# Turning a pass's sums with VectorE instead of TensorE in a three-layer FP32 kernel, with smaller stores and three small moves

## Chip, cores and metric

One core of one Trainium2 chip. The metric is the device time of one execution in microseconds (us), lower is better; the number quoted is the median of the executions shown. Times inside a profile count from the start of the profiled span.

## What is computed

Three layers in FP32, one behind the other; cut to the arithmetic:

```python
# q, k, v: [4, 8, 576, 64], g_norm: [64]
kv  = einsum('bhsd,bhse->bhde', k, v)
o   = einsum('bhsd,bhde->bhse', q, kv)
x   = o / sqrt(mean(o*o, -1) + 1e-6) * g_norm     # -> [2304, 512]
h   = x @ w_in                                    # w_in  [512, 2048]
x   = (h * clip(h + 3, 0, 6) / 6) @ w_out         # w_out [2048, 512]
p   = probs / (probs.sum(-1) + 1e-9)              # probs [2304, 4]
out = sum(p[:, e] * (relu(x @ w1[e]) @ w2[e]) for e in range(4))
# w1 [4, 512, 1024], w2 [4, 1024, 512]
```

## The kernel before

**Precision.** A product is computed as three products of high and low parts, so operands of the matmuls exist twice (`xh`/`xl`, `gH`/`gL`; the two halves of `so`, `tt`, `win`). Parts are made by one ScalarE copy and one VectorE subtraction (`split`, L813 and L814).

**Attention** (`for i in range(NHB)`, eight steps of half a batch each; its first lines are set in a hand-written order under `manual_schedule`). Work on the weights of the second layer is cut into small "conversion parts" (ScalarE copies and VectorE subtractions) that `conv(SLOTS[i])` puts behind step i. After the eight steps come the first products of the second layer (`first_out`), and in front of them four idle 128x128 products of the identity (L586) whose result is not used. Then a short list of second-layer units runs with `conv(NC.pop(0))` behind each, and the domain probabilities are loaded (L615) and normalised by some small VectorE operations (L617 to L630).

**Second layer** (`step`, `second`). While TensorE computes it, `blocks()` reads `w1` and `w2`, forms their sums and differences and parts, and writes them to DRAM as `dwin`, `dtw` and `dwo`. At unit 20 `turn_probs` turns the probabilities on TensorE and writes them to `dpt`.

**Third layer.** Three passes over 768 tokens each; a pass goes through eight groups `g` (numbered 0 to 23 through the passes). A group has two *fronts* k = 2g and 2g+1 and seven *backs* (g, s), s = 0 to 6, of a product scheme with seven instead of eight products. A front has seven products p1, p6, p2, p5, p7, p3, p4 (in this order) of six matmuls of 128x384, between the operands `xs` and one weight load `win` (1.8 MB, two buffers: load k+2 goes out when p4 of front k is done, L967). They go into two PSUM banks, `qa` and `qb` by turns; VectorE and ScalarE take them out, apply the relu and the probabilities and leave `ar`. `prep` makes the back's operand `so` from `ar` (four buffers, one ScalarE copy and one VectorE subtraction of 128x768, and for some backs a VectorE sum before that). A back is 12 matmuls with one `tt` tile (0.5 MB, fed by L974 as tiles come free) into one of the slots `sx`, `sy`, `sz`; `add_out` (L901, L899) adds the slot to the pass's sums `acc2`, which hold output columns in partitions and tokens along the row. Back (g, 0) also has its slot copied to another one by ScalarE (L1085).

**Flush.** At the end of a pass the sums must be turned, so that tokens lie in partitions, and stored. `flush` does this for one quarter (three tiles of tokens, 256 columns) at a time, four times at each of the two boundaries between passes: behind backs s = 2, 5, 6 of the pass's last group (g = 7, 15) and back s = 0 of the next one (g = 8, 16). It issues six TensorE transposes (L919) into a slot, two ScalarE copies into buffers `done` (L923) and six stores of 64 rows by 256 columns (L911). The third pass ends otherwise: its last group turns the sums inside the final products and stores whole rows.

**What sets the order.** In the third layer the instructions are put in order on each engine by the language's scheduler, which has its own idea of costs; the source gives only dependences and a rough order. Every engine then works through its list in order. All loads of this layer and the stores of the flushes go through one queue, SP's (SyncE's). In the built program, each transfer on this queue waits, besides for its data or buffer, for the landing of the transfer that stands eight places ahead of it.

Of the kernel before, what the change touches and what calls it, by code (L numbers as in the profile page):

```python
# [11 lines left out]
AF = mybir.ActivationFunctionType  # L12
# [5 lines left out]
def kernel(  # L18
# [18 lines left out]
    nc = tc.nc  # L37
    B, H, S, D = q.shape
# [471 lines left out]
    nc.scalar.activation(out=gcol, in_=three, func=AF.Sqrt)  # L510
    att_load(1)
    load_raw()
    SLOTS = {0: 7, 1: 2, 2: 3, 3: 0, 4: 2, 5: 1, 6: 3, 7: 0}
    nop = lambda: None
    engines = {
        mybir.EngineType.PE, mybir.EngineType.Activation, mybir.EngineType.DVE, mybir.EngineType.SP}
    with tc.manual_schedule(engines=engines):
# [64 lines left out]
            return lambda: nc.scalar.activation(out=acc[0][:, o, :], in_=po, func=AF.Copy)  # L582

        acc[0] = accp.tile([P, KD, TB], F32, tag="acc", name="acc1")
        for _ in range(4):
            nc.tensor.matmul(kvp[:, 0, :P], lhsT=ident, rhs=ident, start=True, stop=True)  # L586
        d0 = [first_out(o, kvp[:, o]) for o in range(2)]
        for x in d0:
            x()
# [12 lines left out]
        done[0] = True  # L602
        attps.close()
        psb = banks.enter_context(tc.tile_pool(name="psb", bufs=1, space=bass.MemoryType.PSUM, reuse_waits="tile"))
        NC = [4, 4, 4, 3, 3, 0]
        for kind, t in (("o", 1), ("i", 3), ("o", 2), ("i", 4), ("o", 3), ("o", 4)):
            if kind == "i":
                ff_in(0, t, 0)
            else:
                for _ in ff_out(0, t, 0):  # L610
                    pass
            conv(NC.pop(0))
            if t == 2:
                for y in range(2):
                    nc.sync.dma_start(  # L615
                        out=dp[half[y]], in_=moe2_domain_probs.rearrange("(b s j) e -> s b j e", b=B, j=CJ))
        nc.vector.tensor_reduce(out=psum_e, in_=dp, axis=AX.X, op=ALU.add)  # L617
        nc.vector.tensor_scalar(out=psum_e, in0=psum_e, scalar1=1e-9, scalar2=None, op0=ALU.add)
        nc.vector.reciprocal(out=psum_e, in_=psum_e)
# [10 lines left out]
                in1=psum_e[h, y::2, CJ - 1:].to_broadcast([D, 2, E]), op=ALU.mult)  # L630

    TC = DM // 2
    experts = [(e, j) for e in range(E) for j in range(FP)]
    NG = len(experts) // 2
    INPASS = [3, 5, 7, 9, 11, 13]
# [28 lines left out]

    turns = [0]

    def blocks(k, h):

        r = rawt[k, h]
        last = k - 2 * NG + 2 if h else -1  # L670

        def new():
            turns[0] += 1
            z = ring[turns[0] % len(ring)]
            if not isinstance(z, str):
                return z
            return cvp.tile([P, 2, TC], F32R, tag=z, bufs=2 if z == "r" else 1, name="tb")

        def keep(m, src, low, n=2):
            high = new()  # L680
            low = low if low is not None else new()
            hi, lo = high[:, :n], low[:, :n]
            if src is None:
                src = lo.bitcast(F32)
            elif not h:
                hi, lo = (x.rearrange("p m (c f) -> p (m c) f", c=2) for x in (hi, lo))
            nc.scalar.activation(out=hi, in_=src, func=AF.Copy)
            nc.vector.tensor_tensor(out=lo, in0=src, in1=hi.bitcast(F32), op=ALU.subtract)
            for y, x in ((0, high), (1, low)):
                if not h:  # L690
                    nc.sync.dma_start(
                        out=dwin[k][:, y, m:m + n].rearrange("p m c f -> p m (c f)"), in_=x[:, :n].bitcast(F32))
                    continue
                c = min(n, 7 - m) if m else 1
                nc.sync.dma_start(out=dtw[k // 2][:, m:m + c, k % 2, y], in_=x[:, :c].bitcast(F32))
                if last >= 0 and m < 2:
                    nc.sync.dma_start(
                        out=dwo[last][:, int(m > 0), y].rearrange("p (c d) -> p c d", c=2), in_=x.bitcast(F32))

        def sub(out, a, b, op=ALU.subtract):  # L700
            nc.vector.tensor_tensor(out=out, in0=a, in1=b, op=op)

        odd = new()
        od = odd.bitcast(F32)
        if h:
            sub(od, r[:, 1::2], r[:, 0:2])
        else:
            q = r.rearrange("p c (i f) -> p i c f", i=2)
            a11, a12, a21, a22 = (q[:, i, 2 * c:2 * c + 2] for i in range(2) for c in range(2))
            o4 = od.rearrange("p m (c f) -> p m c f", c=2)  # L710
            sub(o4[:, 0], a21, a22, ALU.add)
            sub(o4[:, 1], o4[:, 0], a11)
        yield
        even = new()
        ev = even.bitcast(F32)
        if h:
            sub(ev[:, 0], r[:, 3], od[:, 0])
            sub(ev[:, 1], r[:, 2], ev[:, 0])
        else:
            e4 = ev.rearrange("p m (c f) -> p m c f", c=2)  # L720
            sub(e4[:, 0], a11, a21)
            sub(e4[:, 1], a12, o4[:, 1])
        yield
        keep(3, None, odd)
        yield
        keep(5, None, even)
        yield
        if h:
            keep(1, r[:, 2:4], None)
        else:  # L730
            keep(0, q[:, 0], None)
        yield
        if not h:
            keep(2, a22, None, 1)
        elif last >= 0:
            keep(0, r[:, 0:2], None)
        else:
            keep(0, r[:, 0:1], None, 1)
        rawt.pop((k, h))
        load_rawt()  # L740
        yield
# [27 lines left out]
    for n in range(NB, N3 + 1):  # L769
        step(n)  # L770
        second(n)
        if n == 20:
            turn_probs()
    assert not stream

# [111 lines left out]
    def slot_tile(name):  # L887
        z = slots[0] % 10
        slots[0] += 1
        return (gp if z < 8 else rp).tile([P, TB], F32, tag=("gH", "gL")[z % 2] if z < 8 else "r", name=name)  # L890
# [9 lines left out]
            else:  # L900
                nc.vector.tensor_tensor(out=a, in0=ps[:, d, :TH], in1=a, op=ALU.add)  # L901

    def store(n, src, cols, last=False):
        for y in range(2):
            if n < B * HH:
                b, a = divmod(n, HH)
                j = 4 * (a % 2) + a // 2 + 2 * y
            else:
                b, j = 2 * (n - B * HH) + y, CJ - 1
            queue = nc.scalar if y and last else nc.sync  # L910
            queue.dma_start(  # L911
                out=out.rearrange("(b s j) d -> b j s d", b=B, j=CJ)[b, j][:, cols], in_=src[half[y]])

    def flush(p, th, c, slot):

        part = acc2.pop((th, c))
        for i in range(3):
            for d in range(2):
                nc.tensor.transpose(  # L919
                    slot[:, i // 2, ((i % 2) * 2 + d) * P:((i % 2) * 2 + d + 1) * P], part[d][:, i * P:(i + 1) * P], ident)  # L920
        for i0, n in ((0, 2), (2, 1)):
            t = slot_tile("done")
            nc.scalar.activation(out=t[:, :n * TC], in_=slot[:, i0 // 2, :n * TC], func=AF.Copy)  # L923
            for i in range(n):
                store(rows[p][3 * th + i0 + i], t[:, i * TC:(i + 1) * TC], slice(c * TC, (c + 1) * TC))

    def product(k, bank, m, first):
        n = 0
# [192 lines left out]
    for g in range(NG2 - 1):  # L1121
        nxt = ahead + front(g + 1, 1)
        if (g + 2) % NG == 0 and g + 2 < NG2:
            b = build((g + 2) // NG)
            bld = {2: "5-", 4: "6-", 7: 1, 9: 6, 10: 2, 12: 5, 13: "7-", 15: 7, 16: 3, 17: "4-", 18: 4}
        else:
            bld = {z - 14: m for z, m in bld.items() if z > 13}
        ci = convert_in(2 * g + 3, *halves) if 2 * g + 3 in INPASS else iter(())
        for s in range(7):
            if s < 5:  # L1130
                prep(g, s + 2)
            back(g, s)
            for z in BEHIND[s]:
                nxt[z]()
                if z in bld:
                    b[bld[z]]()
                if z % 2:
                    next(ci, None)
            if g % 2 and s == 3:
                load_probs(g // 2 + 2)  # L1140
            if g % NG == NG - 1 and s in (2, 5, 6):
                flush(g // NG, *((0, 0), (1, 1), (1, 0))[s - 4 if s > 4 else 0], sz if s == 6 else sx)
            if g % NG == 0 and g and s == 0:
                flush(g // NG - 1, 0, 1, sz)
            if s == 5 and g + 1 < NG2 - 1:
                prep(g + 1, 0)
        if g == NG - 1:
            for _ in range(2):
                room(accp, "acc", 2)
        if g + 1 < NG2 - 1:  # L1150
            ahead = front(g + 2, 0)
            ahead[0]()
            prep(g + 1, 1)
# [22 lines left out]
    for z, (jj, i, f) in enumerate(order):  # L1176
# [10 lines left out]
        r = slot_tile("done")  # L1187
        for y in range(2):
            cols = slice(y * TC, (y + 1) * TC)
            if y:  # L1190
                nc.scalar.activation(out=r[:, cols], in_=ps[i][:, cols], func=AF.Copy)
            else:
                nc.vector.tensor_copy(out=r[:, cols], in_=ps[i][:, cols])
        store(rows[NPASS - 1][i], r, slice(0, DM), True)


# [28 lines left out]
```

## Time and profile before

| what | value |
|---|---|
| median of 3 runs | 1172.46 us (1172.0 to 1173.09) |
| the profiled execution | 1172.47 us, of which its span is 1170.7 us |
| TensorE (PE) busy | 1157.8 us, 99% |
| VectorE (DVE) busy | 914.8 us, 78% |
| ScalarE (ACT) busy | 515.2 us, 44% |
| DMA | 279 MB, mean 239 GB/s |

A page of the profile gives busy time by engine, the span in slices, the chain of work that ended last (followed back from the last instruction to whatever released each step), and groups of instructions by source line. Other views list single instructions in a stretch (timeline), what a line's instructions waited for, busy time by stretch (windows) and the transfers with their time from issue to landing. A matmul's record in a timeline is about 0.16 us longer than the distance to the next, since matmuls overlap: distances between starts are what counts.

### The profile page before, as it was taken

The page shows a single profiled execution, that of the slowest core. Times are in us where ns is not written, and L with a number is a line of the kernel's source. Part 1 is how long each engine was busy: PE and PEld are TensorE (multiplying, and loading weights), DVE is VectorE, ACT ScalarE, POOL GpSimd, SP SyncE. Part 2 cuts the span into 40 slices and gives each one's busy share as a digit, 9 for nine tenths or more (in the row PEclk, how much of TensorE's full clock was granted, in tenths as well). Part 3 has the DMA queues.
Part 4 walks back from the last instruction along what each step waited for, and adds up shares of the span by engine and source line. Part 5 has one row for each costly group of instructions (what it writes and reads, how often), then busy time and mean ns, then how long its engine had stood idle before and what let it go on. Part 6 is the DMA issues. An engine that isn't in the chain of part 4 may idle for free.

```text
span 1170.7 us, 19129 instructions
## 1 busy us (share of the span) xinstructions
PE 1157.8 (99%) x7351; PEld 1082.2 (92%) x7351; DVE 914.8 (78%) x1602; ACT 515.2 (44%) x907; POOL 7.6 (1%) x15
## 2 busy tenths in 40 slices
PE   8999999999999999999999999999999999999998
PEld 6788888888888889999999999999999999999996
DVE  5889999977897854788888896777778867777773
ACT  6877555644555532433333444333334443333321
POOL 1100000000000000000000000000000000000000
PEclk9999999999999999999999999999999999999999
DMA  8723267488599552587878789777777887777821
GB/s 313 248 76 115 87 229 282 137 272 262 179 345 379 211 193 94 201 286 272 283 273 295 271 301 327 262 261 268 253 268 252 282 299 273 252 266 252 289 80 54
DMA packets 117219, 279.24 MB, mean 239 GB/s; under 512 B 10176, under 2 KB 69640, under 8 KB 110728
## 3 DMA queue, kind: packets, MB, share of 16 engines
q1 hardware_dynamic: 116644, 277.24, 69.1%
q8 instruction: 58, 0.95, 0.3%
q10 hardware_dynamic: 484, 0.79, 0.2%
q14 instruction: 33, 0.27, 0.1%
HBM read 212.41 MB, written 65.57 MB: 237 GB/s over the span
## 4 chain that ended last, share of the span: by engine, by line
PE 93%; DVE 3%; DMA 2%; ACT 1%; issue 0%; ACTq 0%; SPq 0%; DVEq 0%
PE slot L1078 29%; PE po L402 16%; PE qa L932 15%; PE qb L932 15%; PE ph L367 5%; PE ph L368 5%; PE ph L369 5%; PE slot L1182 1%; DMA kin<-in_k_dram 1%; DMA vin<-in_v_dram 1%; DMA qin<-in_q_dram 1%; DVE xl L323 1%; PE slot L919 0%; PE kvp L254 0%; PE zp L500 0%
## 5 line engine op out<-in xcount | busy, mean ns | idle before, releaser
L1078 PE MATMUL slot<-so,tt 128*128 128x384 f32 x1932 | 362.2, 334 | 0.0
L1078 PEld LDWEIGHTS slot<-so,tt 128*128 128x128 f32 x1932 | 337.0, 188 | 0.0
L932 PE MATMUL qa<-xs,win 128*128 128x384 f32 x1008 | 202.7, 335 | 0.2 <-ACT qa L1016 0.2
L932 PE MATMUL qb<-xs,win 128*128 128x384 f32 x1008 | 201.9, 334 | 0.0
L402 PE MATMUL po<-gH,w 128*128 128x512 f32 (+1 forms) x632 | 191.0, 368 | 0.2 <-ACT gH L383 0.2
L901 DVE TENSOR_TENSOR acc<-slot,acc 128x384 f32<-128x384 f32 x252 | 128.6, 551 | 63.3 <-PE slot L1078 63.1
L932 PEld LDWEIGHTS qa<-xs,win 128*128 128x128 f32 x1008 | 176.9, 188 | 0.9 <-ACT qa L1016 0.5
L932 PEld LDWEIGHTS qb<-xs,win 128*128 128x128 f32 x1008 | 176.9, 188 | 0.3 <-DVE ar L1011 0.2
L813 ACT ACTIVATE so<-ar 128x768 fp32r<-128x768 f32 x142 | 119.4, 844 | 99.3 <-PE slot L1078 52.9
L814 DVE TENSOR_TENSOR so<-ar,so 128x768 fp32r<-128x768 f32 x142 | 133.9, 953 | 25.8 <-ACT so L813 24.6
L402 PEld LDWEIGHTS po<-gH,w 128*128 128x128 f32 x632 | 115.6, 188 | 20.4 <-ACT gH L383 0.6
L367 PE MATMUL ph<-xh,w 128*128 128x512 f32 (+1 forms) x320 | 118.6, 371 | 0.1
L368 PE MATMUL ph<-xl,w 128*128 128x512 f32 (+1 forms) x320 | 117.9, 368 | 0.0
L369 PE MATMUL ph<-xh,w 128*128 128x512 f32 (+1 forms) x320 | 117.8, 368 | 0.0
L402 PE MATMUL po<-gL,w 128*128 128x512 f32 (+1 forms) x316 | 116.4, 368 | 0.0
L380 ACT ACTIVATE r<-ph,three 128x512 f32<-128x512 f32 (+1 forms) x80 | 51.1, 639 | 57.2 <-PE ph L369 56.4
L381 DVE SCALAR_TENSOR_TENSOR r<-r,ph 128x512 f32<-128x512 f32 (+1 forms) x80 | 50.4, 630 | 30.1 <-ACT r L380 29.7
L367 PEld LDWEIGHTS ph<-xh,w 128*128 128x128 f32 x320 | 60.3, 188 | 10.9 <-DVE r L381 0.5
L369 PEld LDWEIGHTS ph<-xh,w 128*128 128x128 f32 x320 | 60.3, 188 | 10.0
L368 PEld LDWEIGHTS ph<-xl,w 128*128 128x128 f32 x320 | 60.3, 188 | 9.9
L402 PEld LDWEIGHTS po<-gL,w 128*128 128x128 f32 x316 | 59.6, 189 | 9.9 <-DVE gL L384 0.2
L1058 DVE TENSOR_TENSOR ar<-ar 128x768 f32<-128x768 f32 x69 | 65.7, 952 | 0.6
(173 smaller groups left out, 1181.4 us busy)
## 6 DMA issues: line engine op xcount, KB each, us to landing
tt<-dtw SPq DMA_DIRECT2D x161, 512.0 KB, 4.8
win<-dwin SPq DMA_DIRECT2D x40, 1792.0 KB, 7.7
dtw<-tb SPq DMA_DIRECT2D x74, 256.0 KB, 4.9
dwin<-win SPq DMA_DIRECT2D x8, 1792.0 KB, 9.2
rawt<-in_moe_w_dram SPq DMA_DIRECT2D x24, 512.0 KB, 4.5
dwin<-tb SPq DMA_DIRECT2D x38, 256.0 KB, 3.4
raw<-in_moe_w_in_dram SPq DMA_DIRECT2D x14, 512.0 KB, 3.8
raw<-in_moe_w_out_dram SPq DMA_DIRECT2D x14, 512.0 KB, 3.5
```

What stands on the lines that cost most here:

```text
L367: nc.tensor.matmul(ph, lhsT=w[:, 0, c, :], rhs=xH[t][:, c, :], start=(c == 0), stop=False)
L368: nc.tensor.matmul(ph, lhsT=w[:, 0, c, :], rhs=xL[t][:, c, :], start=False, stop=False)
L369: nc.tensor.matmul(ph, lhsT=w[:, 1, c, :], rhs=xH[t][:, c, :], start=False, stop=(c == KD - 1))
L380: lambda: nc.scalar.activation(out=r, in_=ph, func=AF.Relu, bias=three[:, 0:1]),
L381: lambda: nc.vector.scalar_tensor_tensor(out=r, in0=r, scalar=6.0, in1=ph, op0=ALU.min, op1=ALU.mult),
L402: nc.tensor.matmul(po_t[u, t][o], lhsT=lhsT, rhs=rhs, start=(f == 0 and m == 0), stop=(f == UF[u] - 1 and m == 2))
L813: nc.scalar.activation(out=dst[0], in_=src, func=AF.Copy)
L814: nc.vector.tensor_tensor(out=dst[1], in0=src, in1=dst[0].bitcast(F32), op=ALU.subtract)
L901: nc.vector.tensor_tensor(out=a, in0=ps[:, d, :TH], in1=a, op=ALU.add)
L932: nc.tensor.matmul(bank, lhsT=w[:, wy, AOP[m], c], rhs=xs[m][:, xy, c], start=first and n == 0, stop=n == 5, skip_group_check=True)
L1058: nc.vector.tensor_tensor(out=dst, in0=a, in1=b, op=op)
L1078: nc.tensor.matmul(slot[:, d, :TH], lhsT=t[:, jj, ty, d * P:(d + 1) * P], rhs=o[:, sy_, jj], start=fresh and m == 0, stop=m == 5, skip_gro ...
```

## The change

1. `flush` turns the sums on VectorE: four operations in 32x32 squares straight from `acc2` to `done` (two of 128x256, two of 128x128, each writing every second element), no TensorE transposes and no ScalarE copies. An operation in squares leaves 32 tokens by 32-column blocks in another arrangement of partitions, so each block of 32 tokens is stored by itself: 12 stores of 4x32x64 in place of six of 64x256. A contiguous piece is then 64 columns, 256 bytes, where it was 1 KB.
2. To have 64 neighbouring columns in one partition row, the columns of `w2` are put apart into even and odd ones when `blocks` reads and converts them (strided reads and writes of the same sizes); the last group's copies undo that (stride 2 in `done`).
3. The conversion parts of attention: step 3 gets one more (0 to 1), step 6 loses its three, the first unit of the drain list has six instead of four.
4. The four idle products are left out.
5. The arithmetic of the probabilities stands behind unit 20 (`set_probs`), no longer in front of the second layer.

Cut to the core:

```diff
-    SLOTS = {0: 7, 1: 2, 2: 3, 3: 0, 4: 2, 5: 1, 6: 3, 7: 0}
+    SLOTS = {0: 7, 1: 2, 2: 3, 3: 1, 4: 2, 5: 1, 6: 0, 7: 0}
...
-        for _ in range(4):
-            nc.tensor.matmul(kvp[:, 0, :P], lhsT=ident, rhs=ident, start=True, stop=True)
...
-        NC = [4, 4, 4, 3, 3, 0]
+        NC = [6, 4, 4, 3, 3, 0]
...
+    def set_probs():
         nc.vector.tensor_reduce(out=psum_e, in_=dp, axis=AX.X, op=ALU.add)
...
+    def apart(t):
+        return t.rearrange("p c (d m) -> p c d m", d=2)
...
+        if h:
+            r = r.rearrange("p c (m d) -> p c d m", d=2)
...
+            if h and src.shape[-1] == P:
+                hi, lo = apart(hi), apart(lo)
...
         if n == 20:
+            set_probs()
             turn_probs()
...
-    def flush(p, th, c, slot):
+    def flush(p, th, c):
 
         part = acc2.pop((th, c))
-        for i in range(3):
+        for i0, n in ((0, 2), (2, 1)):
+            t = slot_tile("done").rearrange("p (b j d) -> p b j d", d=2, j=QP)
             for d in range(2):
-                nc.tensor.transpose(
-                    slot[:, i // 2, ((i % 2) * 2 + d) * P:((i % 2) * 2 + d + 1) * P], part[d][:, i * P:(i + 1) * P], ident)
-        for i0, n in ((0, 2), (2, 1)):
-            t = slot_tile("done")
-            nc.scalar.activation(out=t[:, :n * TC], in_=slot[:, i0 // 2, :n * TC], func=AF.Copy)
+                nc.vector.transpose(
+                    out=t[:, :n * P // QP, :, d],
+                    in_=part[d][:, i0 * P:(i0 + n) * P].rearrange("p (b j) -> p b j", j=QP))
             for i in range(n):
-                store(rows[p][3 * th + i0 + i], t[:, i * TC:(i + 1) * TC], slice(c * TC, (c + 1) * TC))
+                m = rows[p][3 * th + i0 + i]
+                for y in range(2):
+                    for z in range(2):
+                        nc.sync.dma_start(
+                            out=place(m, y)[z * QP:(z + 1) * QP, c * TC:(c + 1) * TC].rearrange(
+                                "i (a f) -> a i f", a=P // QP),
+                            in_=t[:, 4 * i + 2 * y + z].rearrange("p j d -> p (j d)"))
```

What the order of the built programs shows, at the three places that the prediction speaks of. TensorE, first boundary between passes, from p3 of front 19 on (`xs_7139` is p3, `xs_7179` before and `xs_7175` after is p4, `xs_6974` before and `xs_6970` after is p1 of the next front; a row `slot<-so,tt` of 12 matmuls is one back). Before:

```order
L932 MATMUL qa<-xs_7139,win 128x384 x6
L932 MATMUL qb<-xs_7179,win 128x384 x6
L932 MATMUL qa<-xs_6974,win 128x384 x6
L1078 MATMUL slot<-so,tt 128x384 x12
L932 MATMUL qb<-xs_7012,win 128x384 x6
L932 MATMUL qa<-xs_7037,win 128x384 x6
L1078 MATMUL slot<-so,tt 128x384 x12
L932 MATMUL qb<-xs_7075,win 128x384 x6
L932 MATMUL qa<-xs_7129,win 128x384 x6
L1078 MATMUL slot<-so,tt 128x384 x12
```

And of the change, from p4 of front 19 on:

```order
L950 MATMUL qb<-xs_7175,win 128x384 x6
L1096 MATMUL slot<-so,tt 128x384 x48
L950 MATMUL qa<-xs_6970,win 128x384 x6
L1096 MATMUL slot<-so,tt 128x384
L950 MATMUL qb<-xs_7008,win 128x384 x6
L950 MATMUL qa<-xs_7033,win 128x384 x6
L950 MATMUL qb<-xs_7071,win 128x384 x6
L950 MATMUL qa<-xs_7125,win 128x384 x6
L950 MATMUL qb<-xs_7135,win 128x384 x6
L950 MATMUL qa<-xs_7175,win 128x384 x6
L1096 MATMUL slot<-so,tt 128x384 x23
```

Where backs and pairs of products alternated, four backs (9, 0) to (9, 3) now stand in a row behind p4 of front 19, then p1 of front 20, one matmul of the next back, and its other six products. The second boundary has the same piece.

SP's queue from the load of front 18's weights on, first boundary, of the change; before it reads the same, line by line, with `out_dram<-done 64x256 x6` at the four places of the stores:

```order
L985 DMA win<-dwin_1538 128x3584
L940 DMA out_dram<-done 4x32x64 x12
L992 DMA tt<-dtw_1552 128x1024 x3
L940 DMA out_dram<-done 4x32x64 x12
L992 DMA tt<-dtw_1552 128x1024
L985 DMA win<-dwin_1539 128x3584
L940 DMA out_dram<-done 4x32x64 x12
L992 DMA tt<-dtw_1552 128x1024
L992 DMA tt<-dtw_1553 128x1024 x2
L940 DMA out_dram<-done 4x32x64 x12
L992 DMA tt<-dtw_1553 128x1024 x2
L985 DMA win<-dwin_1540 128x3584
```

The order on the queue is kept; the number of stores doubles at each of the four places. The three `tt` rows behind the first stores are the tiles of backs (8, 0) to (8, 2); the last row is the load for front 20.

VectorE at the first flush, of the change (`acc_5374`, `acc_5375` are the two halves of the quarter):

```order
L1029 SCALAR_TENSOR_TENSOR ar<-qb,acc_1530 128x384
L1059 TENSOR_TENSOR cs<-qa,us 128x384
L933 STREAM_TRANSPOSE done<-acc_5374 128x256
L1029 SCALAR_TENSOR_TENSOR ar<-cs,acc_1530 128x384
L933 STREAM_TRANSPOSE done<-acc_5375 128x256
L933 STREAM_TRANSPOSE done<-acc_5374 128x128
L933 STREAM_TRANSPOSE done<-acc_5375 128x128
L824 TENSOR_TENSOR so<-ar,so 128x768
```

The turning stands between a front's relu and the subtraction for a back's operand; before, nothing of the flush was on this engine.

## Rows read from the trace of the kernel before

**Rows 1.** The page's busy times, TensorE first.

```profile
PE 1157.8 (99%) x7351; PEld 1082.2 (92%) x7351; DVE 914.8 (78%) x1602; ACT 515.2 (44%) x907; POOL 7.6 (1%) x15
```

**Rows 2.** The page's chain that ended last, by engine.

```profile
PE 93%; DVE 3%; DMA 2%; ACT 1%; issue 0%; ACTq 0%; SPq 0%; DVEq 0%
```

**Rows 3.** Groups by line and form: count, then busy us, mean ns, idle.

```profile
L919 PE MATMUL slot<-ident,acc 128*128 128x128 f32 x48 | 6.5, 272 | 0.0
...
L586 PE MATMUL kvp<-ident 128*128 128x128 f32 x8 | 1.1, 274 | 0.0
```

**Rows 4.** TensorE's timeline around one flush: start, us, instruction.

```profile
704.20 1.20 PE L932 MATMUL qb<-xs,win 128*128 128x384 f32 x6
705.24 0.82 PE L919 MATMUL slot<-ident,acc 128*128 128x128 f32 x6
705.81 1.31 PE L932 MATMUL qa<-xs,win 128*128 128x384 f32 x6
```

**Rows 5.** The end of attention, timeline.

```profile
62.04 0.70 ACT L168 ACTIVATE r<-raw 128x512 uint32<-128x512 uint32 x1
...
64.15 1.05 PE L586 MATMUL kvp<-ident 128*128 128x128 f32 x8
```

**Rows 6.** VectorE's group by form that is nearest to the new operations.

```profile
L1193 DVE COPY done<-slot 128x256 f32<-128x256 f32 x6 | 2.6, 425 | 13.1 <-PE slot L1182 13.1
```

**Rows 7.** Windows, three flushes: PE, PEld, DVE, ACT, POOL, clock, DMA share, GB/s.

```profile
694.15:723.25 29.10, 29.10 (x176) 29.00 (x175) 21.27 (x33) 13.69 (x26) 0.00 (x0) 1.00 0.90 306
```

**Rows 8.** Timeline, p4 of front 19 and the two backs after it.

```profile
734.69 1.20 PE L932 MATMUL qb<-xs,win 128*128 128x384 f32 x6
...
735.73 1.20 PE L932 MATMUL qa<-xs,win 128*128 128x384 f32 x6
...
736.77 2.24 PE L1078 MATMUL slot<-so,tt 128*128 128x384 f32 x12
...
737.00 0.47 ACT L1016 ACTIVATE qb<-qa 128x384 f32<-128x384 f32 x1 [2.28 <-PE qa L932]
...
738.85 1.20 PE L932 MATMUL qb<-xs,win 128*128 128x384 f32 x6
...
739.15 0.96 DVE L814 TENSOR_TENSOR so<-ar,so 128x768 fp32r<-128x768 f32 x1
...
740.93 2.24 PE L1078 MATMUL slot<-so,tt 128*128 128x384 f32 x12
```

**Rows 9.** SP's queue, timeline: a weight load, stores, the next weight load.

```profile
689.66 0.32 SPq L967 DMA_DIRECT2D win<-dwin  x1
690.07 4.20 SPq L911 DMA_DIRECT2D out_dram<-done  x6
...
701.87 3.67 SPq L911 DMA_DIRECT2D out_dram<-done  x6
...
720.86 0.38 SPq L967 DMA_DIRECT2D win<-dwin  x1
```

**Rows 10.** Issue time on SP by line: form, ns least/median/most.

```profile
L615 SPq DMA_DIRECT2D dp<-in_moe_domain_probs_dram x2: 618/684/749, 81.9 to 82.7; - x2
```

**Rows 11.** Waits of SP's queue from 688 to 724: total us, times, longest.

```profile
SPq L974 <- DMA win<-dwin: 6.8, 2, 3.8
```

**Rows 12.** DMA issues: count, KB each, median us from issue to landing.

```profile
tt<-dtw SPq DMA_DIRECT2D x161, 512.0 KB, 4.8
win<-dwin SPq DMA_DIRECT2D x40, 1792.0 KB, 7.7
...
out_dram<-done SPq DMA_DIRECT2D x48, 64.0 KB, 5.8
```

**Rows 13.** The page's busiest queue; a window of small pieces.

```profile
q1 hardware_dynamic: 116644, 277.24, 69.1%
...
330.00:360.00 30.00, 30.00 (x135) 24.82 (x133) 28.23 (x53) 18.14 (x33) 0.00 (x0) 1.00 1.05 368
```

**Rows 14.** Its packets, from the DMA view of that window.

```profile
DMA packets 10401, 11.04 MB, mean 368 GB/s; under 512 B 669, under 2 KB 9375, under 8 KB 10399
```

More of the change, by code (lines that the diff above doesn't have):

```diff
@@ L632 @@
     TC = DM // 2
+    QP = 32
     experts = [(e, j) for e in range(E) for j in range(FP)]
@@ L705, in blocks @@
         if h:
-            sub(od, r[:, 1::2], r[:, 0:2])
+            sub(apart(od), r[:, 1::2], r[:, 0:2])
         else:
@@ L716, in blocks @@
         if h:
+            od, ev = apart(od), apart(ev)
             sub(ev[:, 0], r[:, 3], od[:, 0])
@@ L901, in add_out, with place, store @@
                 nc.vector.tensor_tensor(out=a, in0=ps[:, d, :TH], in1=a, op=ALU.add)
-    def store(n, src, cols, last=False):
-        for y in range(2):
[L905 to L912, printed above, removed]
-    def flush(p, th, c, slot):
+    def place(n, y):
+        if n < B * HH:
+            b, a = divmod(n, HH)
+            j = 4 * (a % 2) + a // 2 + 2 * y
+        else:
+            b, j = 2 * (n - B * HH) + y, CJ - 1
+        return out.rearrange("(b s j) d -> b j s d", b=B, j=CJ)[b, j]
+    def store(n, src):
+        for y in range(2):
+            queue = nc.scalar if y else nc.sync
+            queue.dma_start(out=place(n, y), in_=src[half[y]])
+    def flush(p, th, c):
         part = acc2.pop((th, c))
-        for i in range(3):
+        for i0, n in ((0, 2), (2, 1)):
+            t = slot_tile("done").rearrange("p (b j d) -> p b j d", d=2, j=QP)
             for d in range(2):
-                nc.tensor.transpose(
-                    slot[:, i // 2, ((i % 2) * 2 + d) * P:((i % 2) * 2 + d + 1) * P], part[d][:, i * P:(i + 1) * P], ident)
-        for i0, n in ((0, 2), (2, 1)):
-            t = slot_tile("done")
-            nc.scalar.activation(out=t[:, :n * TC], in_=slot[:, i0 // 2, :n * TC], func=AF.Copy)
-            for i in range(n):
-                store(rows[p][3 * th + i0 + i], t[:, i * TC:(i + 1) * TC], slice(c * TC, (c + 1) * TC))
+                nc.vector.transpose(
+                    out=t[:, :n * P // QP, :, d],
+                    in_=part[d][:, i0 * P:(i0 + n) * P].rearrange("p (b j) -> p b j", j=QP))
+            for i in range(n):
+                m = rows[p][3 * th + i0 + i]
[5 more added lines that the diff above has]
+                            in_=t[:, 4 * i + 2 * y + z].rearrange("p j d -> p (j d)"))
     def product(k, bank, m, first):
@@ L1141 @@
             if g % NG == NG - 1 and s in (2, 5, 6):
-                flush(g // NG, *((0, 0), (1, 1), (1, 0))[s - 4 if s > 4 else 0], sz if s == 6 else sx)
+                flush(g // NG, *((0, 0), (1, 1), (1, 0))[s - 4 if s > 4 else 0])
             if g % NG == 0 and g and s == 0:
-                flush(g // NG - 1, 0, 1, sz)
+                flush(g // NG - 1, 0, 1)
             if s == 5 and g + 1 < NG2 - 1:
@@ L1189 @@
             cols = slice(y * TC, (y + 1) * TC)
+            o = r[:, cols].rearrange("p (m d) -> p d m", d=2)
+            z = ps[i][:, cols].rearrange("p (d m) -> p d m", d=2)
             if y:
-                nc.scalar.activation(out=r[:, cols], in_=ps[i][:, cols], func=AF.Copy)
+                nc.scalar.activation(out=o, in_=z, func=AF.Copy)
             else:
-                nc.vector.tensor_copy(out=r[:, cols], in_=ps[i][:, cols])
-        store(rows[NPASS - 1][i], r, slice(0, DM), True)
+                nc.vector.tensor_copy(out=o, in_=z)
+        store(rows[NPASS - 1][i], r)
 _INS = ['q', 'k', 'v', 'g_norm', 'moe_w_in', 'moe_w_out', 'moe2_domain_probs', 'moe2_w1', 'moe2_w2']
```

## Prediction

> **What bounds the kernel now.** I read the page first. TensorE is busy for 99% of the span [rows 1], and the chain that ended last runs over it for 93%, with 3% on VectorE [rows 2]. So a change counts in two ways only: TensorE work that goes away, and waits of TensorE that come or go; work added elsewhere costs nothing until TensorE waits for it. The granted clock in the windows is 1.00 [rows 7, 13], so TensorE runs at its upper level (2.4 GHz) in them; nothing here idles it for more than a few us at a time, and I expect no other. The profiled execution took 1172.47 us with a span of 1170.7; the sum is made against 1172.5, which is also the median of the runs. A measurement tells about 0.2%, 2.3 us, from no change.
>
> **TensorE's part of the flush.** The timeline around a flush shows what the six transposes take of the path [rows 4]: a product starts at 704.20, the transposes at 705.24 (1.04 later, a product's own length), and the next product at 705.81, so 0.57 by starts; the back behind the next product then starts 1.14 instead of 1.04 later, 0.10 more. One flush is 0.67 us, eight are **-5.4 us**. The busy sum of the group, 6.5 [rows 3], counts overlap twice.
>
> **Attention.** Four idle products (eight matmul records) last 1.05 us from 64.15 [rows 5], but PE waits for ScalarE and VectorE there, so that most of it becomes a wait. What does shorten the path is a conversion copy (0.70 us from 62.04) that stands in front of the copies of attention's last step; without step 6's parts these start some 0.6 us earlier. I take **-0.6 us**, bounds 0 and -1.05. Clock: the gap that the idle products filled is about one us, and I expect no fall. The parts moved to step 3 and the drain list, strided conversions of the same sizes, and the probabilities' arithmetic (needed only by the turning at unit 20, long after) stand beside a TensorE that has its operands, VectorE at 78% and ScalarE at 44% [rows 1]: nothing, within 0.5 either way.
>
> **VectorE's part of the flush.** No row shows a turning in squares. The nearest is a copy of 128x256 at 0.425 us [rows 6]; I take that for 128x256 and, between it and nothing, about 0.3 for 128x128: 1.45 us a flush. The stretch with three flushes has 29.10 - 21.27 = 7.8 us of idle VectorE [rows 7], against 4.4 added, so I cost it at nothing. The cover is thin at the first flush, where four operations stand between a front's relu and a back's operand: at twice the price it is gone, and PE waits 1.5 us or so at each flush (2 x 4 x 1.5 = 12, the upper bound). Below nothing is excluded: nothing goes away on VectorE.
>
> **Backs in a row.** The order on TensorE changes at both boundaries. Before, p4 of front 19 starts at 734.69, p1 of front 20 at 735.73, back (9, 0) at 736.77, two products, and back (9, 1) at 740.93 [rows 8]. The operand of (9, 1) is ready when VectorE's subtraction ends, 739.15 + 0.96 = 740.11, that is 5.42 us after p4's start; it hangs on p4 itself. In the new order nothing lies between p4, back (9, 0) and back (9, 1): the latter could start 1.04 + 2.08 = 3.12 us after p4's start. PE waits 5.42 - 3.12 = **2.3 us**. The other backs' operands follow at the pace of PE. Then p1 of front 20 is followed by a single matmul of a back (0.17) and p6, which needs ScalarE's copy of p1's result: it starts at 737.00 and lasts 0.47, where p1 started at 735.73, so 1.74 after p1's start, while p6 could start 1.04 + 0.17 = 1.21 after. That is 0.5 more: about 2.8 per boundary, **+5.5 us** for two. Lower bound 0 (if another chain had the operand ready earlier), upper 7.4 (2.8 + 0.85 for one more ScalarE copy in front of the operand's).
>
> **Stores on SP's queue.** Six stores take 3.67 us of issue, 0.61 each [rows 9]. A store of 4x32x64 has 128 pieces instead of 64; the load of the probabilities, in far smaller pieces, takes 0.62 to 0.75 [rows 10], so I keep 0.61. Twelve stores take 7.3 us. Each transfer also waits for the landing of the one eight ahead; that the tile loads waited 6.8 us for weight loads here [rows 11] is this rule at work. First flush: the weight load goes out at 689.66 and lands 7.7 later [rows 9, 12], 697.7 with its issue; the stores start at about 691 (690.07 before, and VectorE ends a little later than ScalarE did); the eighth, which would go at 695.3, waits until 697.7, and the rest takes until 700.7. The tile of back (8, 0) then goes out at 701.1 and lands 4.8 later [rows 12], at 705.9. That back starts at 706.95 in the trace, less three flushes' 0.67, at 704.9: **1.0 us late**. At the third flush, which stands behind load 19, the same happens; load 20 went out at 720.86 [rows 9], with 735.73 - 721.24 - 7.7 = 6.8 us to spare, and the new order wants it some 10 us later still, while SP loses 14.7 us more to issues and 5 to such waits, against gaps in its list of 10 to 13. Between 0 and 1.8 late; I take 0.9. Sum **+3.8 us** for both boundaries, bounds 0 and 8.
>
> **Sum.** 1172.5 - 5.4 - 0.6 + 5.5 + 3.8 = **1175.8 us**, slower by 0.28%. Own range 1173 to 1179.
>
> **Price of a small piece.** The page's busiest queue had 116,644 packets of 2377 bytes on average in 69.1% of sixteen engines' 1170.7 us, 111 ns each; a window of small ones 10,401 of 1061 bytes in 1.05 of 16 x 30 us, 48.5 ns [rows 13, 14]. Both are 0.046 ns per byte, by which 256 bytes take 12 ns; 48.5 is the upper end. Spread over 16 engines, a boundary's 48 x 128 pieces are 4.6 us per engine at 12 ns, as much as before for the same bytes.
>
> **Rivals.**
>
> *The stores overload few engines* (0.25). If a store ran on 4 engines, 48 x 32 = 1536 pieces would queue on each: 18.4 us at 12 ns, 74.5 at 48.5. Transfers take 0.90 of the engines in this stretch [rows 7]; over 75 us (I give it two and a half groups to even out) that leaves 7.5, and load 20 has 6.8 us of lead (above): 14.3 us fit in, and from 14.3 / 1536 = 9.3 ns on loads come late. At 16 ns (a third above the byte price, for the smallness) it is 24.6 - 14.3 = 10.3 per boundary, in place of the 1.9 above and of some 1.5 of the backs' wait: 1175.8 - 3.8 - 3 + 20.6 = 1190. For it: the outermost dimension of the new store's target is 4. Against: no transfer in this trace is of that shape. The Trainium skill (DMA: Bandwidth & Descriptors, the section on why a DMA increments its semaphore by 16 and not by 1) says that the number of engines is the largest number up to 16 that divides the slowest dimension of both patterns, here 4 for 4 and 128. By that rule this rival's first condition holds; no run here has shown it.
>
> *The saving stays, the waits don't come* (0.15; the other side). Place: the operand of back (9, 1) and the tile of (8, 0). VectorE is idle for 7.8 of 29.1 us and SP has gaps; if the operand's chain runs 2.3 us ahead of the old one, because p1's result and its copies no longer stand between, and tiles land in 3.3 rather than 4.8, then 1172.5 - 6.0 = 1166.5, with part of the waits up to 1170. It decides from 1.8 us of wait per boundary downward.
>
> *Loads in time, backs wait* (0.20). As forecast, but the eight-ahead rule costs nothing that PE sees: 1172.5 - 6.0 + 5.5 = 1172.0. The change then does on TensorE what it says and gets nothing.
>
> **Chances.** The forecast has 0.40. Below 1170.1 lies the second rival: faster 0.15. Within 2.3 us lie the third and a little of the forecast (0.05): 0.25. Slower is 0.35 + 0.25 = 0.60. The range takes in half of the second rival and most of the first: 1168 to 1194.
>
> **What would show it.** In the changed profile: no L919 on TensorE; the four backs in a row with a wait of 2 to 3 us before the second, for a subtraction on VectorE; back (8, 0) waiting about 1 us for a tile; weight loads at 7 to 8 us. The first rival shows as `tt` and `win` landing times of 12 us and more and waits of PE for DMA of 5 us and more; turnings above 0.6 us for 128x256 would bring waits for VectorE at the flushes. The forecast is wrong if PE waits for nothing at (9, 1), or if waits lie outside the two boundaries.

## Result and the profile after

| | before | change |
|---|---|---|
| median, us (6 runs each) | 1172.78 | 1183.64 (1180.67 to 1185.38) |
| ratio, 95% interval | 1 | 1.0087 (1.0072 to 1.0103) |
| profiled execution, us | 1172.47 | 1183.88, span 1182.1 |
| mean granted clock of the span | 0.999 | 0.995 |

Slower by 0.9%, about 10 us; the forecast said slower, by 0.28%, with a range that holds the result. From the page of the change, against [rows 1, 2]: busy times, chain, and two groups by line:

```profile
PE 1159.3 (98%) x7295; PEld 1079.9 (91%) x7295; DVE 923.5 (78%) x1634; ACT 508.9 (43%) x891; POOL 7.6 (1%) x15
...
PE 91%; DMA 4%; DVE 2%; SPq 1%; ACT 1%; issue 0%; ACTq 0%; DVEq 0%
...
L1096 PE MATMUL slot<-so,tt 128*128 128x384 f32 x1932 | 365.7, 336 | 6.3 <-ACT so L823 3.4
...
L402 PE MATMUL po<-gH,w 128*128 128x512 f32 (+1 forms) x632 | 191.4, 368 | 1.2 <-ACT gH L383 1.2
```

TensorE is busy for longer although 48 transposes and the four idle products (eight records) are gone, and transfers (4%) and SP's queue (1%) are on the chain. The backs wait 6.3 us where they waited for nothing worth a row. Where the time lies, by the first product of the third layer (450.7 before, 453.1 now) and its last (1144.9, 1155.9): 2.4 us arise ahead of it, 8.6 in it. All waits of TensorE in the third layer are at the two boundaries, but for 0.2 us that it also had before. From TensorE's timeline at the first one (start, length, instruction, in brackets the idle time before it and what ended it):

```profile
706.13 1.21 PE L950 MATMUL qa<-xs,win 128*128 128x384 f32 x6
709.06 2.35 PE L1096 MATMUL slot<-so,tt 128*128 128x384 f32 x12 [1.72 <-DMA tt<-dtw]
...
737.56 2.24 PE L1096 MATMUL slot<-so,tt 128*128 128x384 f32 x12
741.49 0.44 PE L1096 MATMUL slot<-so,tt 128*128 128x384 f32 x1 [1.69 <-ACT so L823]
742.48 7.91 PE L1096 MATMUL slot<-so,tt 128*128 128x384 f32 x35 [0.55 <-DVE so L824]
751.03 1.32 PE L950 MATMUL qa<-xs,win 128*128 128x384 f32 x6 [0.64 <-DMA win<-dwin]
752.34 0.41 PE L1096 MATMUL slot<-so,tt 128*128 128x384 f32 x1
752.91 1.31 PE L950 MATMUL qb<-xs,win 128*128 128x384 f32 x6 [0.16 <-ACT qb L1034]
```

The first line with a bracket is back (8, 0), late for its tile. Then four backs stand in a row: 12 matmuls, a wait of 1.69 for the operand of (9, 1), and 36 more; behind them front 20 waits for its weights. The waits add up to 4.8 us here and 2.9 at the second boundary. One thing is not a wait: 35 matmuls take 7.91 us, where 35 at the old distance (twelve in 2.08) take 6.07 and the 0.16 of a record's end. The windows show why (columns as in [rows 7]):

```profile
742.00:744.00 2.00, 1.52 (x7) 1.52 (x8) 2.00 (x3) 1.64 (x3) 0.00 (x0) 0.89 0.86 264
744.00:746.00 2.00, 2.00 (x8) 2.00 (x8) 1.50 (x3) 0.46 (x1) 0.00 (x0) 0.50 1.12 467
746.00:748.00 2.00, 2.00 (x11) 2.00 (x10) 1.43 (x3) 0.38 (x1) 0.00 (x0) 0.76 1.05 441
748.00:750.00 2.00, 2.00 (x13) 2.00 (x12) 1.65 (x3) 0.00 (x0) 0.00 (x0) 1.00 0.88 370
```

After TensorE had stood for 1.69 and 0.55 us with one matmul between, its granted clock falls to 0.50, the lower level of 1.2 GHz, for some 3 us; that costs 7.91 - 6.07 - 0.16 = 1.7 us more.

SP's queue through the first boundary, against [rows 9]:

```profile
693.67 11.53 SPq L940 DMA_DIRECT2D out_dram<-done  x12
705.30 1.36 SPq L992 DMA_DIRECT2D tt<-dtw  x3
706.75 9.81 SPq L940 DMA_DIRECT2D out_dram<-done  x12
716.67 0.41 SPq L992 DMA_DIRECT2D tt<-dtw  x1
717.18 0.38 SPq L985 DMA_DIRECT2D win<-dwin  x1
717.64 11.95 SPq L940 DMA_DIRECT2D out_dram<-done  x12
729.70 1.36 SPq L992 DMA_DIRECT2D tt<-dtw  x3
731.16 9.49 SPq L940 DMA_DIRECT2D out_dram<-done  x12
740.76 0.89 SPq L992 DMA_DIRECT2D tt<-dtw  x2
741.74 0.38 SPq L985 DMA_DIRECT2D win<-dwin  x1
```

A single store's issue is 0.54 us at the median, yet twelve take 9.5 to 12 here, 42.8 us at the four places where the old stores took 15.3. The rest is waiting inside a few issues: in seven of the eight flushes the fifth store's issue takes 2.5 to 4.3 us (behind a weight load the third's or fourth's can be long too), and the seven behind it pass at about 0.58 each. Here is the last flush above, split, then the DMA engines' packets from 731 to 736 and from 738 to 740.5, and the window of the latter:

```profile
731.16 2.47 SPq L940 DMA_DIRECT2D out_dram<-done  x4
733.67 2.86 SPq L940 DMA_DIRECT2D out_dram<-done  x1
736.58 4.08 SPq L940 DMA_DIRECT2D out_dram<-done  x7
```
```profile
DMA packets 411, 1.50 MB, mean 301 GB/s; under 512 B 44, under 2 KB 44, under 8 KB 411
DMA packets 721, 0.18 MB, mean 72 GB/s; under 512 B 721, under 2 KB 721, under 8 KB 721
738.00:740.50 2.50, 1.80 (x11) 1.48 (x9) 2.50 (x5) 0.60 (x1) 0.00 (x0) 1.00 0.32 72
```

A store has 128 pieces of 256 bytes. From 731 to 736 only 44 packets are that small, so no store moved: the transfer eight places ahead of the fifth store, the last store of the flush before, was done, and the four stores just issued had not begun. The fifth store's issue ends when they do (542 packets under 512 bytes from 736 to 738). So this is not the wait for a landing eight places ahead that the prediction counted. Why SP gets no further than four isn't shown.

Load 20 goes out at 741.74, 20.9 us later than before; 2.3 of these were there at load 18 already (691.93, before 689.66). VectorE's new operations, by form:

```profile
L933 DVE STREAM_TRANSPOSE done<-acc 128x256 f32<-128x256 f32 x16 | 6.7, 431 | 0.0
L933 DVE STREAM_TRANSPOSE done<-acc 128x128 f32<-128x128 f32 x16 | 4.0, 280 | 0.0
```

### The profile page after: what moved, and what is told of

Read it like the earlier page. It is cut to its first block, busy times and chain, and to the rows that moved or that the text cites. A ratio compares the mean times of both kernels' runs of the same rounds, so it can differ in the third digit from the quotient of the medians.

```text
span 1182.1 us, 19119 instructions
## 1 busy us (share of the span) xinstructions
PE 1159.3 (98%) x7295; PEld 1079.9 (91%) x7295; DVE 923.5 (78%) x1634; ACT 508.9 (43%) x891; POOL 7.6 (1%) x15
## 2 busy tenths in 40 slices
DMA packets 126051, 279.23 MB, mean 236 GB/s; under 512 B 22080, under 2 KB 78472, under 8 KB 119560
## 4 chain that ended last, share of the span: by engine, by line
PE 91%; DMA 4%; DVE 2%; SPq 1%; ACT 1%; issue 0%; ACTq 0%; DVEq 0%
PE slot L1096 26%; PE po L402 16%; PE qa L950 14%; PE qb L950 14%; PE ph L367 5%; PE ph L369 5%; PE ph L368 5%; DMA win<-dwin 1%; PE slot L1200 1%; SPq L940 1%; DMA qin<-in_q_dram 1%; DMA kin<-in_k_dram 1%; DMA vin<-in_v_dram 1%; DMA tt<-dtw 1%; PE zp L500 0%
## 5 line engine op out<-in xcount | busy, mean ns | idle before, releaser
L402 PE MATMUL po<-gH,w 128*128 128x512 f32 (+1 forms) x632 | 191.4, 368 | 1.2 <-ACT gH L383 1.2
L402 PEld LDWEIGHTS po<-gH,w 128*128 128x128 f32 x632 | 115.6, 188 | 21.5 <-ACT gH L383 1.8
L402 PE MATMUL po<-gL,w 128*128 128x512 f32 (+1 forms) x316 | 116.5, 369 | 0.2 <-DVE gL L384 0.2
L402 PEld LDWEIGHTS po<-gL,w 128*128 128x128 f32 x316 | 59.6, 189 | 10.5 <-DVE gL L384 0.7
```

Of the source, the lines that this page charges most:

```text
L402: nc.tensor.matmul(po_t[u, t][o], lhsT=lhsT, rhs=rhs, start=(f == 0 and m == 0), stop=(f == UF[u] - 1 and m == 2))
```

## Experiments

Theory: the third layer loses, by what the stores do to SP's queue, by the order of backs that comes with them, and by the clock after long waits. Rivals: VectorE's work; the attention part; the small pieces themselves, wherever they stand. Ratios are against the kernel before, run on the same chip.

**flush_only** undoes the attention part of the change:

```diff
-    SLOTS = {0: 7, 1: 2, 2: 3, 3: 1, 4: 2, 5: 1, 6: 0, 7: 0}
+    SLOTS = {0: 7, 1: 2, 2: 3, 3: 0, 4: 2, 5: 1, 6: 3, 7: 0}
...
+        for _ in range(4):
+            nc.tensor.matmul(kvp[:, 0, :P], lhsT=ident, rhs=ident, start=True, stop=True)
...
-        NC = [6, 4, 4, 3, 3, 0]
+        NC = [4, 4, 4, 3, 3, 0]
...
-    def set_probs():
...
-            set_probs()
```

> The change without its attention part: steps' conversion parts, idle products and the probabilities' place as before, flush and stores as in the change. Third layer to blame (backs in a row, late loads, and the lower clock after them; 8.6 of the 11.0 us lie between its first and last product in the profile): 1172.8 + 8 to 9 = about 1181 us, with the same waits at the two boundaries. If the attention part is to blame for most: 1176 us or less.

1181.82 us, ratio 1.0082 (1.0068 to 1.0096). The loss is the flush's; the attention part is not told from nothing beside it. Most runs below start from this kernel.

**attn_only** is the reverse, the attention part on the kernel before.

> The kernel before with the attention part alone (conversion parts, no idle products, probabilities' arithmetic later). By the forecast's term: -0.6 us, 1172.2. By the profile of the change: the end of attention about 0.9 shorter, but two waits of TensorE for gH behind the first unit of the drain list, which has six parts now, 1.2 us; the rest of the 2.4 us ahead of the third layer was a lower clock from 16 to 20 us, which either kernel can meet: 1172.5 to 1174. If the part really costs 2.4: 1175.

1173.60 us, ratio 1.0007 (0.9998 to 1.0016): no gain. TensorE's waits show the new one, which was 0.2 before:

```profile
PE po L402 <- ACT gH L383: 1.2, 2, 0.7
```

**attn_nc2** moves its two additional conversion parts behind the next unit:

```diff
-        NC = [6, 4, 4, 3, 3, 0]
+        NC = [4, 6, 4, 3, 3, 0]
```

> As attn_only, but the two parts more of the drain list stand behind its second unit, not its first. If these two parts in front of gH's copies are the 1.2 us of wait: no wait for gH beyond 0.2, 1172.3 us. If the wait comes from elsewhere: as attn_only, 1173.6.

1172.81 us, ratio 1.0003 (0.9994 to 1.0012). The wait for `gH` is gone from the list (one of 0.5 us for a ScalarE copy, L422, has come in); the time agrees with a us gained over attn_only, but the intervals overlap, so that only the wait is shown.

**no_stores** takes flush_only's stores out (the first two passes' output is left out):

```diff
-                for y in range(2):
-                    for z in range(2):
-                        nc.sync.dma_start(
...
+                pass
```

> As flush_only without any store in the flushes (the first two passes' output is left out); regular order on TensorE. This is the flush on VectorE alone. By the forecast's terms: 1172.8 - 5.4 = 1167.4 us, no wait at the boundaries and the clock at 1.00 there. If VectorE's operations cost TensorE waits: 1169 or more.

1167.16 us, ratio 0.9953 (0.9941 to 0.9965), that is -5.5 us against -5.4 forecast. Order regular, and at the first boundary TensorE is busy throughout at full clock, with 6 us more on VectorE than before in the same stretch (62.74 then):

```profile
685.00:770.00 85.00, 85.00 (x492) 85.00 (x492) 68.81 (x120) 30.18 (x51) 0.00 (x0) 1.00 0.82 285
```

So the turning on VectorE is free, and all of the loss, some 15 us, comes with the stores.

**quarter_stores** keeps 12 issues a flush, each with a quarter of the pieces and other dimensions (three quarters of the first two passes' output left out):

```diff
-                            out=place(m, y)[z * QP:(z + 1) * QP, c * TC:(c + 1) * TC].rearrange(
-                                "i (a f) -> a i f", a=P // QP),
-                            in_=t[:, 4 * i + 2 * y + z].rearrange("p j d -> p (j d)"))
+                            out=place(m, y)[z * QP:(z + 1) * QP, c * TC:c * TC + 2 * QP],
+                            in_=t[:QP, 4 * i + 2 * y + z].rearrange("p j d -> p (j d)"))
```

> As flush_only, but a store takes only the 32 partitions of one column block, so 12 stores of 32x64 a flush: the same number of issues on SP, a quarter of the pieces, and an outermost dimension of 32. Three quarters of the first two passes' output are left out. The order on TensorE is the regular one of before. If pieces on few engines and the backs in a row are the cause: no waits at the boundaries, 1172.8 - 5.4 = 1167.4 us. If the number of issues on SP's queue is the cause: back (8, 0) still waits 1 to 2 us for its tile at both boundaries, 1170 to 1172. If VectorE's operations are the cause: 1173 or more, with waits for VectorE.

1177.77 us, ratio 1.0044 (1.0032 to 1.0057). The expectation was wrong about the order: the four backs in a row are there. Loads are nearly in time (0.2 us of waiting for a tile in all), so this run shows what the order costs by itself. TensorE's waits from 680 to 770, and the slow matmuls behind them:

```profile
PE slot L1094 <- ACT so L822: 1.7, 1, 1.7
PE slot L1094 <- DVE so L823: 0.5, 1, 0.5
PE qb L948 <- ACT qb L1032: 0.4, 1, 0.4
PE slot L1094 <- DMA tt<-dtw: 0.2, 1, 0.2
```
```profile
739.26 7.94 PE L1094 MATMUL slot<-so,tt 128*128 128x384 f32 x35 [0.55 <-DVE so L823]
```

Between no_stores and this lie 10.6 us: 5.2 of waits at both boundaries (idle TensorE: 2.8 and 2.4), 3.5 of low clock (35 matmuls in 7.94 and 8.02), the rest not placed. Between this and flush_only lie 4 us: late tiles and weights (waits of 4.4 us there, 0.2 here). A store's longest issue is 1.4 us here, and the wait for a landing eight places ahead shows outside the issues; SP's waits from 684 to 765 have this row, where the change's name no transfer that a store waited for:

```profile
SPq L939 <- DMA win<-dwin: 7.6, 2, 3.9
```

**regular** writes TensorE's order by hand for the groups around the boundaries:

```diff
+        with (tc.manual_schedule(engines={mybir.EngineType.PE}) if g in (7, 8, 9, 15, 16, 17) else nullcontext()):
...
```

> As flush_only, but TensorE's order is written by hand for the groups around the boundaries: backs and fronts alternate as before, no four backs in a row. If the order itself is the cost (waits for operands 5 us and the lower clock after them 3.4 in both boundaries): 1181.8 - 8 = about 1173.5 us. If the late loads are the cost and the scheduler's order covered one of them: load 20 lands at about 751 in the profile of flush_only's kind, and the regular order wants it at about 740, so TensorE waits about 10 us for it at each boundary: 1190 us or more.

1196.42 us, ratio 1.0207 (1.0188 to 1.0226). Undoing the order alone is worse by some 15 us than leaving it, since front 20 then needs its weights before they are there:

```profile
747.08 2.26 PE L949 MATMUL qa<-xs,win 128*128 128x384 f32 x6 [9.26 <-DMA win<-dwin]
```

At the second boundary the same product waits 6.1 us, by the profile for VectorE, and at both the six matmuls behind the wait take 2.26 us instead of 1.20, the low clock again (0.92 and 0.94 from 685 to 770 and from 945 to 1030). The scheduler's order was a cover: four backs in front of the product that would wait. The two costs aren't to be had singly; both hang on the stores.

**half_act** lets ScalarE's queue issue six of the twelve:

```diff
-                        nc.sync.dma_start(
+                        (nc.scalar if y else nc.sync).dma_start(
```

> As flush_only, but six of the 12 stores of a flush are issued by ScalarE's queue, so that SP issues six as before; the order on TensorE is the regular one. If SP's issues and its rule of eight in flight make the loads late: 1172.8 - 5.4 + up to 2 for ScalarE's issues (0.5 each) = 1167 to 1170 us. If the four engines' load of small pieces makes them late: waits for tiles and weights stay, 1172 to 1185.

1197.53 us, ratio 1.0209 (1.0195 to 1.0223), outside both cases. TensorE waits for no weights; but SP's own waits now name weight loads for 9.3 us, in two stores:

```profile
SPq L939 <- DMA win<-dwin: 9.3, 2, 4.8
```

And the stores on ScalarE wait for those ahead, and what ScalarE should do for the fronts waits behind them (waits of TensorE):

```profile
PE qb L949 <- ACT us L1045: 8.9, 2, 4.5
PE qa L949 <- ACT us L1037: 5.5, 2, 2.8
PE qb L949 <- ACT qb L1033: 4.7, 2, 3.0
```

**gp_stores** lets GpSimd issue all twelve:

```diff
-                        nc.sync.dma_start(
+                        nc.gpsimd.dma_start(
```

> As flush_only, but the 12 stores of a flush (all of the output) are issued by GpSimd, so SP's queue holds loads alone, and the regular order of backs stands on TensorE. If SP's queue (issues and transfers behind one another) and the order are the cause: 1167 to 1168 us. If the 256-byte pieces take the loads' engines whatever the queue: waits for tiles or weights remain, 1170 to 1178, with landing times above those of before.

1326.24 us, ratio 1.1307 (1.1291 to 1.1322), far outside. GpSimd's timeline has one store every 2.7 us, 0.7 of it busy:

```profile
723.69 0.69 POOL L939 DMA_DIRECT2D out_dram<-done  x1 [1.99 <-issue]
726.42 0.70 POOL L939 DMA_DIRECT2D out_dram<-done  x1 [2.04 <-issue]
729.17 0.69 POOL L939 DMA_DIRECT2D out_dram<-done  x1 [2.06 <-issue]
```

48 stores take 130 us so; the buffers that the next pass's sums need come free that late, and a product waits up to 56.5 us. It tells nothing of the pieces.

**spread** keeps the change's stores on SP, but puts four behind each back instead of twelve in a row:

```diff
-                        nc.sync.dma_start(
+                        late.append((
...
+            for _ in range(4):
+                if late:
+                    o, i = late.pop(0)
+                    nc.sync.dma_start(out=o, in_=i)
```

> As flush_only with the change's own stores (4x32x64, 48 per boundary), but four behind each back instead of twelve in a row, so that the next tile's load stands behind four at most. The scheduler doubles up two backs here and there, not four. If a row of twelve on the queue makes the loads late: 1168 to 1172 us. If four engines can't carry the pieces beside the loads (2.2 us per back at 17 ns a piece, beside 0.8 of 4.2 us for the loads): loads run late by about a us per back until the last store, 1178 or more.

1175.69 us, ratio 1.0030 (1.0018 to 1.0042), between the two cases. Half of flush_only's loss and more goes. What is left are two backs in a row in several places (waits of 1.5 and 1.7 for their operands) and two short waits for weights, with the clock at 1.00 throughout.

**staged** gives the stores another shape. A flush writes its two buffers as they are to a scratch in DRAM, and copies from DRAM to DRAM bring them to the output, one behind each back of the next groups:

```diff
+            nc.sync.dma_start(
+                out=stage[p][th, c][:, 4 * i0:4 * (i0 + n)], in_=t[:, :4 * n].rearrange("p b j d -> p b (j d)"))
...
-                        nc.sync.dma_start(
+                        late.append((
...
+                            stage[p][th, c][:, 4 * (i0 + i) + 2 * y + z].rearrange("(a i) f -> i a f", i=QP)))
...
+            if late and g % NG < NG - 1 and (g % NG or s):
+                o, i = late.pop(0)
+                nc.sync.dma_start(out=o, in_=i)
```

> As flush_only, but a flush writes its two buffers to a scratch in DRAM (one store of 128x512, one of 128x256: pieces of 2 KB and 1 KB, 128 partitions outermost), and 48 copies from DRAM to DRAM per boundary (32x4x64, outermost 32) bring it to the output later, one behind each back of the next groups; regular order on TensorE. If the stores' place and shape on SP's queue are the whole loss: near no_stores, 1167 to 1168.5 us, faster than both kernels, no wait at the boundaries. If 256-byte pieces disturb the loads wherever they stand: 1170 or more, with waits spread over the groups after a boundary.

1166.14 us, ratio 0.9944 (0.9931 to 0.9956): faster than the kernel before by 6.5 us and than the change by 17. TensorE is busy throughout both boundaries at full clock, its list of waits has none in the third layer above 0.2 us, and the loads land as before [rows 12]:

```profile
685.00:770.00 85.00, 85.00 (x493) 85.00 (x492) 68.82 (x121) 30.51 (x50) 0.00 (x0) 1.00 0.88 309
```
```profile
tt<-dtw SPq DMA_DIRECT2D x161, 512.0 KB, 5.1
win<-dwin SPq DMA_DIRECT2D x40, 1792.0 KB, 7.6
...
out_dram<-stage SPq DMA_DIRECT2D x96, 32.0 KB, 6.0
```

The 96 copies have the same 128 pieces of 256 bytes each. So small pieces as such don't cost. This run changes the stores' place on the queue and their shape together, so it doesn't say which of the two did how much; no issue of a copy is longer than 1.6 us.

**staged_attn** adds the attention part of attn_nc2 to it.

> staged with the attention part of attn_nc2 (parts moved, the two more behind the drain list's second unit, no idle products, probabilities later). If the two add up: staged's 1166.1 less the 0.5 that attn_nc2 stood below before: 1165.6 us. If the attention part gives nothing, as its interval there says: 1166.1, the difference within 1 us either way.

1166.98 us, ratio 0.9949 (0.9936 to 0.9963): nothing gained.

**On how many engines a store ran.** Each transfer's end leaves small packets beside its data, and the packet counts give their number. The DMA view's line of no_stores, the kernel before, the change, quarter_stores and staged, in this order:

```profile
DMA packets 113378, 276.08 MB, mean 237 GB/s; under 512 B 9408, under 2 KB 65800, under 8 KB 106888
```
```profile
DMA packets 117219, 279.24 MB, mean 239 GB/s; under 512 B 10176, under 2 KB 69640, under 8 KB 110728
```
```profile
DMA packets 126051, 279.23 MB, mean 236 GB/s; under 512 B 22080, under 2 KB 78472, under 8 KB 119560
```
```profile
DMA packets 117987, 276.88 MB, mean 235 GB/s; under 512 B 14016, under 2 KB 70408, under 8 KB 111496
```
```profile
DMA packets 129507, 282.38 MB, mean 242 GB/s; under 512 B 23488, under 2 KB 80904, under 8 KB 123016
```

Without any of these stores 9408 packets under 512 bytes remain. The kernel before has 768 more, 48 x 16: its pieces are of 1 KB, so each old store left 16 end packets. The change adds 96 x 128 pieces of 256 bytes, 12288, and 22080 - 9408 - 12288 = 384 = 96 x 4. With 32 as the outermost dimension, quarter_stores gives 14016 - 9408 - 96 x 32 = 1536 = 96 x 16, and staged (with 16 scratch stores) 23488 - 9408 - 12288 = 1792 = 112 x 16. So the change's stores ended on 4 engines, the others on 16. The counts agree with the rule of the Trainium skill (DMA: Bandwidth & Descriptors, the section on why a DMA increments its semaphore by 16 and not by 1), which the prediction could cite but no run had shown. What the pieces took is in the rows of 738 to 740.5 above, where nothing but such stores moved: 721 packets in 2.5 us are one every 13.9 ns on each of four engines, and 72 GB/s. Twelve stores put 384 pieces on each, 5.3 us at that pace.

## Why the prediction was right, and where not

The direction was forecast, the size was not: +3.3 us against about +10. The forecast's own range, 1173 to 1179, does not hold the measured 1183.6; the wider one, 1168 to 1194, does, because it was stretched for the first rival, so this is luck in part. And by a sign that it set itself the forecast was wrong in one place: there is a wait outside the two boundaries, 1.2 us for `gH`.

- **TensorE's part, -5.4:** right. no_stores measures -5.5 (-6.9 to -4.1).
- **Attention, -0.6:** the step failed. The tail did shorten: from the last of attention's large group of transposes (L330) to the first unit of the drain list (L402) 6.4 us passed instead of 7.4 (64.6 to 71.0, before 62.6 to 70.0). But "nothing, within 0.5 either way" for the parts moved to the drain list overlooked that ScalarE makes `gH` there in between: 1.2 us of waits, as attn_only shows and attn_nc2 takes away. The rest of the 2.4 us ahead of the third layer is mostly a low clock in this one execution (0.63 and 0.52 granted from 16 to 20 us, 1.00 before); in the medians flush_only and the change lie 1.8 us apart, with intervals that overlap.
- **VectorE's part, 0:** right, with 0.431 and 0.280 us against 0.425 and 0.3.
- **Backs in a row, +5.5:** the waits were right (forecast 2.8 a boundary, measured 2.4 and 2.1), though most of the wait before the second back was for ScalarE's copy (1.69), and VectorE's subtraction held up only the second matmul (0.55, at the first boundary alone). The failed step is on the clock: "nothing here idles it for more than a few us at a time, and I expect no other". About two were enough, at both boundaries of the profile, for 1.7 and 1.6 us on top.
- **Stores on SP's queue, +3.8:** near in sum (waits for tiles and weights 2.3 and 0.8; quarter_stores against flush_only 4 us), wrong in the reason. The sum had 14.7 us of issues and 5 of waits for weight loads eight places ahead, 19.7 a boundary. The queue shows 27.5 (42.8 against 15.3), and the waits are the long issues of the fifth stores, behind tiles as well as behind weight loads. Counted from load 18, load 20 went out 18.6 us later. The order wanted it later too, so that TensorE waited only 0.6 and 0.2 for weights, where the sum had 0.9 a boundary; without that cover it was 9.3 at the first boundary (regular).
- **Rival of few engines:** its condition holds (4 engines). With the measured 13.9 ns a piece its sum gives 1536 x 13.9 = 21.3 less 14.3, so 7.0 a boundary and 1183.0 in all. That this lies next to the measured 1183.6 is chance, since its waits did not come: TensorE waited 3.2 us for transfers, not 14, and load 20 landed 9.3 us after it went out (741.74 to 751.03), not 12 or more. What does go with the four engines are the long issues: no store or copy that ran on 16 engines has one over 2 us. Their effect on time isn't separated: spread has the same stores on the same engines and recovers 6 us by their place and the order that follows from it, quarter_stores 4 us with a quarter of the pieces on 16.
- **Where the other 7 us are:** forecast +3.3, measured about +10.2 by the ratio. Low clock 3.3, the attention part some 1 where -0.6 was forecast; the waits came out at 7.7 for a forecast of 9.3. About 4 us aren't placed.

## What to carry to other kernels

Work that is moved off one engine can cost more on a queue than it saved: count the transfers that stand in front of the next load, how long each holds the queue and on how many engines it runs, not their bytes. When a scheduler answers a change with a new order, ask what it was covering before undoing it; here the order cost some 10 us, and taking it away another 15. Work that must be stored in small pieces can be parked in large ones first and spread over a quiet stretch: that kept all of the saving.

## What the runs showed of the hardware that I had not expected

- TensorE's granted clock fell to 0.50 for some 3 us after waits of 1.7 and 0.3 to 0.6 us with a single matmul between them (the change and quarter_stores, both boundaries; flush_only, the first). In flush_only's second boundary, with 1.7 and 0.5, it stayed at 1.00 (35 matmuls in 6.33 us); what decides between them isn't settled.
- A store from GpSimd came every 2.7 us, with 0.69 of it busy, where SP issued the same one in 0.54.
- Stores on four engines moved at 72 GB/s, a 256-byte piece every 13.9 ns on each, with 0.32 of the engines' time; SP issued four of them while the loads ahead were still moving, and the fifth's issue lasted until the first ones' pieces moved (2.5 to 4.3 us in seven of eight flushes).
- Turning in 32x32 squares with writes of every second element runs at the speed of a plain copy of the same size (0.431 us for 128x256, a copy 0.425).
